# Dealing TensorE fill to attention steps by each step's own matmul work

## The chip, the cores and the metric

One Trainium2 chip; the kernel runs on one core. The metric is device time in microseconds (us) of one execution, median of several. PE is TensorE, DVE is VectorE, ACT is ScalarE, POOL is GpSimd and SP is SyncE. TensorE's clock has two levels here, 2.4 GHz (granted clock 1.00) and 1.2 GHz (0.50).

## The reference

Thresholded attention for 2 batches x 8 heads, sequence 576, head width 64; its output, 1152 tokens of 512, passes through two layers of experts, 8 and then 4, each expert 512 to 1024 to 512 and computed for all tokens.

```python
def _attn_ref(q, k, v, tau):
    scores = scale * np.matmul(q, k.transpose(0, 1, 3, 2))
    thresh = np.max(scores, axis=-1, keepdims=True) - tau
    scores = np.where(scores >= thresh, scores, -1000000000.0)
    scores = scores - np.max(scores, axis=-1, keepdims=True)
    attn = np.exp(scores)
    attn = attn / (np.sum(attn, axis=-1, keepdims=True) + 1e-09)
    return np.matmul(attn, v).astype(np.float32)
...
    for e in range(E):                       # first layer, P: gate, normalized by rows and columns 8 times
        h = np.maximum(x @ w1[e], 0.0)
        out += P[:, e:e + 1] * (h @ w2[e])
...
    for e in range(E):                       # second layer, p: given probabilities, normalized by row
        h = np.maximum(x @ w1[e], 0.0)
        out += p[:, e:e + 1] * (h @ w2[e])
```

## The kernel before

The queries of the 16 head-and-batch pairs are cut into 72 **units** of up to 128 queries. `Attention.step` (L396) is one step of a software pipeline and works on several units at once: at step time `t` it transposes the normalized weights of unit t-2, masks and reduces unit t and t+1, computes the scores of unit t+2, and, where a group of 320 or 256 queries is complete, multiplies its weights with the values (`mix`, nine matmuls into a PSUM tile `pv`). The program's order on each engine is the order in which this Python code is written; nothing reorders it. In this text a step has the number k of the unit that it transposes, so k = t-2, and it begins with PE's transposes of that unit (tiles `et` and `er`, L313 and L315).

In a step, PE has: five transposes; **fill, phase 0**; scores (L271, four matmuls, eight in a few steps); `pv` (L355, L357) in some steps; **fill, phase 1**. ACT has: the copy of `et` out of PSUM (`hi`, L320, and of a finished `er`, L322), the copy of a finished `pv` (`out`, L374), the relu of a fill group that ended in phase 0 (L474), the exponential (L291), the relu of a group that ended in phase 1, and then preparation for coming heads (casts of keys, values, queries and weights: L71, L239, L240, L96). DVE has: mask (L295), maximum (L276), three small ones, then `lo` (L330 and, for a finished `er`, L333), then what lies in the list `later`: the `rest` of `pv` (L377), and `hl` of a fill group (L477).

**Fill** is expert work of the first layer that is ready before all heads are (`expert_fill`, L457): tokens of batch 0 first, 256 and then 320 columns at a time. It is a generator that yields after each **piece**. A layer-1 group (L468) has three pieces of four matmuls and accumulates in one PSUM bank; its bank comes free when ACT's relu and DVE's `hl`, which subtracts the relu's result from the sum, have read it. A layer-2 group (L495) has twelve pieces of two matmuls 512 columns wide; its bank comes free with ACT's copy L499. `pv` of attention takes its tile from the same pool `ps_m`, which has **two banks**; the other six banks are scores (four), `et` (one) and `er` (one). A `pv` bank comes free with `out` on ACT and `rest` on DVE, which stand in the step after the one that filled it.

Fill begins at k=18 and stops about k=33, when its first batch of work is used up; the second batch begins at k=38. The dealing is in `fill` and `pull` (L563 to L583): `pull(3)` in phase 0 of every step; in phase 1, when a group is still open or the step has no `pv`, more pieces up to 3 (or 4 in the second batch).

Of the kernel before, what the change touches and what calls it, by code (L numbers as in the profile page):

```python
# [22 lines left out]
NT = N // P  # L23
HS = S // 2
BIG = 3.0e38
RA1, RA2 = 3, 4


@with_exitstack
def attention_two_moe_kernel(ctx, tc, qP, kP, qT, kT, vp, tau, wg, w1, w1s, w2, dp, m2w1s, m2w2, out):  # L30
# [80 lines left out]
    class Attention:  # L111
# [5 lines left out]
        def __init__(self, pl, ps_s, ps_t, ps_r, ps_m):  # L117
            self.pl, self.ps_s, self.ps_t, self.ps_r, self.ps_m = pl, ps_s, ps_t, ps_r, ps_m
            self.units, self.heads = [], []
            self.t = -2  # L120
            self.work = {}
            self.later, self.late = [], []
            self.iq = self.iv = self.lq = self.lv = 0
            self.xf = {}
            self.eth = pl.tile([P, 5, 640], F32R, name="eth")
            self.e32 = pl.tile([P, 5, 512], F32, tag="etl", name="e32")
            self.etl = None
            self.qz = [pl.tile([P, 3 * D], F32R, name=f"qz{i}") for i in range(2)]
            for z in self.qz:
                V.tensor_scalar(z[:, D:2 * D], ident[:, :D], 0.0, None, op0=ALU.mult)  # L130
# [208 lines left out]
        def mix(self, g, part):  # L339
            hd, n, c = g["head"], g["n"], slice(g["c"], g["c"] + g["n"])  # L340
            if part == 0:
                g["pv"] = self.ps_m.tile([P, 512], F32, tag="mm", name="pv")
            pv = g["pv"]
            if hd["exact"]:
                r0 = (hd["h"] % 2) * D
                for kt in self.parts(hd)[part]:
                    k = P if kt < 4 else D
                    T.matmul(pv[r0:r0 + D, :n], lhsT=hd["v"][:k, kt], rhs=self.e32[:k, kt, c], start=kt == 0,  # L348
                             stop=kt == 4)
                if part == 2:  # L350
                    self.lv -= 1
            elif part == 0:
                vf = hd["vs"].rearrange("p a b c -> p a (b c)")
                for kt in range(4):
                    T.matmul(pv[:, :n], lhsT=vf[:, kt], rhs=self.etl[:, kt, c], start=kt == 0, stop=False)  # L355
                for kt in range(5):
                    T.matmul(pv[:, :n], lhsT=vf[:, kt], rhs=self.eth[:, kt, c], start=False, stop=kt == 4)  # L357

        def out(self, g):
            hd, n, pv, pl = g["head"], g["n"], g["pv"], self.pl  # L360
            h, t0 = hd["h"], hd["b"] * S + g["q0"]
            r0 = (h % 2) * D
            r, kt, c = slice(r0, r0 + D), h // 2, slice(t0, t0 + n)
            if hd["exact"]:
                A.copy(xh[r, kt, c], pv[r, :n])
                self.later.append(lambda: V.tensor_tensor(xl[r, kt, c], pv[r, :n], f(xh[r, kt, c]), op=ALU.subtract))
                return

            key = hd["h"] // 2, g["n"]
            if key not in self.xf:  # L370
                self.xf[key] = pl.tile([P, n], F32, tag=f"xf{n}", name="xf", bufs=1)
            xf = self.xf[key]
            o = slice(D - r0, 2 * D - r0)
            A.copy(xf[r, :n], pv[o, :n])  # L374

            def rest():
                V.tensor_tensor(xf[r, :n], pv[r, :n], xf[r, :n], op=ALU.add)  # L377
                if "half" in self.xf.setdefault(key + ("n",), {}):
                    del self.xf[key], self.xf[key + ("n",)]
                    self.late.append(lambda: split(A, G, xh[:, kt, c], xl[:, kt, c], xf[:, :n]))  # L380
                else:
                    self.xf[key + ("n",)]["half"] = True

            self.later.append(rest)
# [11 lines left out]
        def step(self, fill, side):  # L396

            us, t = self.units, self.t
            un = lambda i: us[i] if 0 <= i < len(us) else None
            self.load()  # L400
            nxt, a, d, x, c, z, y = (un(t + i) for i in (2, 1, 0, -2, -3, -4, -5))
            if x:
                self.turn(x)
            if d:
                self.mask(d)
            if a:
                self.top(a)
            if d:
                self.guard(d)
            if a:  # L410
                self.line(a)
            if d:
                self.norm(d)
            for part, u in ((2, y), (1, z), (0, c)):
                for g in u["mix"] if u else ():
                    if g["head"]["exact"]:
                        self.mix(g, part)
            if x:
                self.hi(x)
            for u, late in ((z, False), (y, True)):  # L420
                for g in u["mix"] if u else ():
                    if late == (g["head"]["exact"] and g["head"]["h"] < H - 1):
                        self.out(g)
            fill(0, bool(c and c["mix"]))
            if a:
                self.exp(a)
            if x:
                self.lo(x)
            if nxt:
                self.scores(nxt)  # L430
            self.run(self.later)
            for g in c["mix"] if c else ():
                if not g["head"]["exact"]:
                    self.mix(g, 0)
            fill(1, bool(c and c["mix"] or z and z["mix"]))
            self.run(self.late)
            for w in self.work.pop(t, ()):
                w()
            side()
            self.t += 1  # L440
            return self.t < len(us) + 5
# [15 lines left out]
    def expert_fill(hp, w, n0, n, cols, dst, tail, q0, later, free):  # L457

        hs = []
        for ft in range(FT):
            wh, wl = w.w1(ft)
            ph = bank()
            ops = [(wl, xh), (wh, xl), (wh, xh)]
            for i, (a, x) in enumerate(ops):
                for kt in range(KT):
                    T.matmul(ph[:, :n], lhsT=a[:, kt * P:(kt + 1) * P], rhs=x[:, kt, n0:n0 + n],  # L468
                             start=i == 0 and kt == 0, stop=i == 2 and kt == KT - 1)
                if i < 2:  # L470
                    yield 2 - i
            hh = hp.tile([P, n], F32R, tag="hh", name="hh", bufs=FT)
            hl = hp.tile([P, n], F32R, tag="hl", name="hl", bufs=FT)
            A.activation(hh, ph[:, :n], AF.Relu)  # L474

            def low(hh=hh, hl=hl, ph=ph, ft=ft):
                V.scalar_tensor_tensor(hl, ph[:, :n], 0.0, f(hh), op0=ALU.max, op1=ALU.subtract)  # L477
                if tail is not None:
                    for h, to in zip((hh, hl), tail):
                        for q, c in enumerate((0, n - 32)):  # L480
                            G.tensor_scalar(to[:, ft, (q0 + q) * 32:(q0 + q + 1) * 32], f(h[:, c:c + 32]), 1.0, 1.0,
                                            op0=ALU.mult, op1=ALU.mult)

            later.append(low)
            hs.append((hh, hl))
            free(1)
            yield 0
        for t, c in cols:
            py = bank()
            i = 0  # L490
            for ft in range(FT):
                (hh, hl), (wh, wl) = hs[ft], w.w2(ft)
                hh, hl = (x[:, c:c + P] for x in (hh, hl)) if t < NT - 1 else (x[:, ft] for x in tail)
                for x, a in ((hl, wh), (hh, wl), (hh, wh)):
                    T.matmul(py, lhsT=x, rhs=a, start=i == 0, stop=i == 3 * FT - 1)  # L495
                    i += 1
                    if i % 2 == 0 and i < 3 * FT:
                        yield 12 - i // 2
            A.copy(dst[t], py)  # L499
            yield 0  # L500
        free(FT)

    def keep(n):
        pass
# [9 lines left out]
    with ExitStack() as att:  # L514
# [45 lines left out]

        left, spent = [0], [0]

        def pull(n, end=True):  # L563

            for i in range(n):
                if not todo or at.t <= todo[0][0] or (left[0] == 1 and not end):
                    return i
                left[0] = next(todo[0][1], -1)
                if left[0] < 0:
# [3 lines left out]
                    return i + 1  # L573
            return n

        def fill(phase, busy):
            if phase == 0:
                if 0 <= at.t < nA0 - 3 and at.t % 2 == 0:
                    room[0] -= 1
                    cook()  # L580
                spent[0] = pull(3)
            elif left[0] or not busy:
                pull(max((RA1 if at.t < nA1 + 3 else RA2) - spent[0], 0), True)  # L583

        while at.step(fill, side):
            pass
# [168 lines left out]
    def scale():  # L755

        for t in (0, 1, 2, 3, 4, 5, 6, 7, 8):
            e = int(t > 3)
            V.tensor_scalar(acc[t], acc[t], p1[:, t, e:e + 1], None, op0=ALU.mult)
            if t < 4:  # L760
                V.scalar_tensor_tensor(acc[t], y1[t], p1[:, t, 1:2], acc[t], op0=ALU.mult, op1=ALU.add)
# [324 lines left out]
```

## Time and profile before

| what | value |
|---|---|
| median of 3 runs | 1345.97 us (1344.51 to 1347.28) |
| the profiled execution's own time | 1345.91 us |
| its span in the profile | 1344.1 us (1.8 us outside it) |
| PE busy | 1316.8 us, 98% of the span |
| DVE, ACT, POOL busy | 50%, 42%, 52% of the span |
| steps k=18 to 32 | 65.18 to 115.17 us |
| steps k=33 to 37 | 115.17 to 130.23 us |
| steps k=38 to 70 | 130.23 to 245.40 us |

A step's start is the start of its first transpose L313 on PE. The steps with fill are a sixth of the span; the rest is expert work, whose matmuls follow one another closely.

### The profile page before, as it was taken

To read this page: it belongs to the slowest core of one execution; us is meant where nothing else is said; L and a number is where in the kernel's file an instruction comes from. 1 tells how busy PE (TensorE), PEld (TensorE's weight loads), DVE (VectorE), ACT (ScalarE), POOL (GpSimd) and SP (SyncE) were. 2 spreads that over 40 slices of the span, in tenths; PEclk is the share of its full clock that TensorE was granted. 3 is DMA by queue.
4 is the path that set the end of the run, shared out by engine and by line. 5 is a ranking of instruction groups with operands and counts; after the bars stand their busy time and mean duration, and the time that the engine had idled before them with its cause. 6 is when DMAs were issued, how large, how long until landed. Compare 5 with 4: busy or idle time off the path is not lost.

```text
span 1344.1 us, 20909 instructions
## 1 busy us (share of the span) xinstructions
PE 1316.8 (98%) x7777; PEld 1164.7 (87%) x7777; DVE 670.9 (50%) x1526; ACT 567.4 (42%) x1300; POOL 696.8 (52%) x837
## 2 busy tenths in 40 slices
PE   8998999999999999999999999999899999999998
PEld 5697988899889889898898989888789889898987
DVE  5798888356863434343343433434334334343343
ACT  6887786333444324242332423335434233242321
POOL 6886975442875335434543643544963454364330
PEclk9999999999999999999999999999999999999999
DMA  5542330100321112011111201101101111120101
GB/s 156 162 125 65 104 94 17 32 24 25 103 71 39 48 40 63 24 56 48 31 50 47 63 25 56 48 25 55 48 24 56 48 32 50 46 63 25 32 9 63
DMA packets 42054, 73.58 MB, mean 55 GB/s; under 512 B 5088, under 2 KB 10336, under 8 KB 41952
## 3 DMA queue, kind: packets, MB, share of 16 engines
q1 hardware_dynamic: 41664, 71.96, 18.0%
q8 instruction: 61, 1.00, 0.3%
q14 instruction: 41, 0.34, 0.1%
q10 hardware_dynamic: 288, 0.28, 0.1%
HBM read 69.86 MB, written 2.36 MB: 54 GB/s over the span
## 4 chain that ended last, share of the span: by engine, by line
PE 90%; DVE 3%; ACT 3%; POOL 3%; issue 1%; DMA 0%; POOLq 0%; ACTq 0%; DVEq 0%
PE mm L1003 38%; PE mm L893 33%; PE mm L468 5%; PE mm L495 5%; PE sc L271 2%; PE et L313 2%; PE pv L348 2%; PE pv L357 1%; PE pv L355 1%; DVE ex L295 1%; DVE etl L330 1%; POOL wl L76 1%; DVE st L276 1%; ACT ex L291 0%; ACT eth L320 0%
## 5 line engine op out<-in xcount | busy, mean ns | idle before, releaser
L1003 PE MATMUL mm<-wh,hs 128*128 128x512 f32 x1344 | 435.4, 397 | 2.0 <-DVE hs L869 2.0
L76 POOL TENSOR_TENSOR wl<-raw,wh 128x512 fp32r<-128x512 f32 x154 | 199.3, 1307 | 337.1 <-ACT wh L71 335.0
L1003 PEld LDWEIGHTS mm<-wh,hs 128*128 128x128 f32 x1344 | 252.3, 188 | 64.1 <-DVE hs L869 8.3
L1011 DVE SCALAR_TENSOR_TENSOR acc<-mm,p,acc 128x512 f32<-128x512 f32 x181 | 135.7, 750 | 300.7 <-PE mm L1003 300.7
L1003 PE MATMUL mm<-wl,hs 128*128 128x512 f32 x672 | 264.1, 393 | 0.0
L898 ACT COPY s<-mm 128x288 f32<-128x288 f32 x84 | 33.6, 401 | 450.4 <-PE mm L893 450.4
L869 DVE SCALAR_TENSOR_TENSOR hs<-mm,hs 128x288 fp32r<-128x288 f32 x252 | 114.8, 456 | 103.5 <-ACT hs L868 103.1
L1003 PEld LDWEIGHTS mm<-wl,hs 128*128 128x128 f32 x672 | 126.6, 188 | 27.2
L893 PE MATMUL mm<-xh,wl 128*128 128x288 f32 x672 | 144.3, 296 | 2.4 <-ACT w L898 1.4
L893 PE MATMUL mm<-xl,wh 128*128 128x288 f32 x672 | 143.8, 295 | 0.0
L893 PE MATMUL mm<-xh,wh 128*128 128x288 f32 x672 | 143.8, 295 | 0.0
L76 POOL TENSOR_TENSOR wl<-ws,wh 128x512 fp32r<-128x512 f32 x88 | 115.8, 1319 | 36.4 <-ACT wh L71 26.7
L868 ACT ACTIVATE hs<-mm 128x288 fp32r<-128x288 f32 x252 | 104.2, 414 | 69.5 <-DVE mm L920 64.7
L893 PEld LDWEIGHTS mm<-xh,wl 128*128 128x128 f32 x672 | 110.1, 189 | 7.0 <-ACT w L898 1.9
L893 PEld LDWEIGHTS mm<-xh,wh 128*128 128x128 f32 x672 | 108.1, 188 | 0.0
L893 PE MATMUL mm<-xth,wl 128*128 128x288 f32 x504 | 107.9, 295 | 0.0
L893 PEld LDWEIGHTS mm<-xl,wh 128*128 128x128 f32 x672 | 107.9, 188 | 0.0
L893 PE MATMUL mm<-xth,wh 128*128 128x288 f32 x504 | 107.7, 295 | 0.0
L893 PE MATMUL mm<-xtl,wh 128*128 128x288 f32 x504 | 107.7, 295 | 0.0
L875 POOL TENSOR_SCALAR ht<-hs 128x128 fp32r<-128x128 f32 x168 | 49.7, 302 | 111.1 <-ACT hs L868 96.2
L71 ACT CAST wh<-raw 128x512 fp32r<-128x512 f32 x154 | 95.7, 623 | 13.5 <-PE mm L893 10.4
L631 POOL TENSOR_TENSOR ws<-raw 128x512 f32<-128x512 f32 x44 | 57.6, 1309 | 53.9 <-DMA raw<-in_w1s 31.0
(172 smaller groups left out, 2299.2 us busy)
## 6 DMA issues: line engine op xcount, KB each, us to landing
raw<-in_w SPq DMA_DIRECT2D x88, 256.0 KB, 3.0
raw<-in_w1s SPq DMA_DIRECT2D x56, 256.0 KB, 2.7
raw<-in_m2w1s SPq DMA_DIRECT2D x32, 256.0 KB, 2.7
raw<-in_m2w SPq DMA_DIRECT2D x32, 256.0 KB, 2.9
kr<-in_kT SPq DMA_DIRECT2D x22, 288.0 KB, 2.9
vr<-in_vp SPq DMA_DIRECT2D x24, 160.0 KB, 2.3
qr<-in_qT SPq DMA_DIRECT2D x8, 288.0 KB, 2.8
out_y<-acc SPq DMA_DIRECT2D x8, 256.0 KB, 2.0
```

What stands on the lines that cost most here:

```text
L71: A.copy(hi, src)
L76: el.tensor_tensor(lo, src, f(hi), op=ALU.subtract)
L468: T.matmul(ph[:, :n], lhsT=a[:, kt * P:(kt + 1) * P], rhs=x[:, kt, n0:n0 + n], start=i == 0 and kt == 0, stop=i == 2 and kt == KT - 1)
L495: T.matmul(py, lhsT=x, rhs=a, start=i == 0, stop=i == 3 * FT - 1)
L631: G.tensor_tensor(s, a, b, op=op)
L868: A.activation(hh, src, AF.Relu)
L869: V.scalar_tensor_tensor(hl, src, 0.0, f(hh), op0=ALU.max, op1=ALU.subtract)
L875: G.tensor_scalar(tail[j][:, :, q:q + 32], f(side[s][j][:, :, 2 * P:]), 1.0, 1.0, op0=ALU.mult, op1=ALU.mult)
L893: T.matmul(m, lhsT=w[:, (2 * g + kt) * P:(2 * g + kt + 1) * P], rhs=operand(u, kt, lo), start=first and j == 0, stop=j == len(ops) - 1, sk ...
L898: A.copy(z[name], m)
L1003: T.matmul(py, lhsT=hs[x][:, k, o:o + P], rhs=w, start=n == 0, stop=n == 3 * HF - 1)
L1011: V.scalar_tensor_tensor(acc[t], py, s, acc[t], op0=ALU.mult, op1=ALU.add)
```

## The change

A step gets a budget in place of a fixed number. At phase 0 the program adds up the step's own PE work in nanoseconds (`own`: 550 for the transposes, 530 for each group of scores, four for each column of `pv`) and adds (3300 - own)/480 pieces to what the step before left over, of which at most one piece is carried. Up to 3 whole pieces are dealt in phase 0 and the rest in phase 1. A new group is not begun while more than one of the two banks has users whose releasing instructions are not yet written (`later` and the new counter `open`). Two lines keep the scaling of a result from being written before the fill that makes that result (`written`).

```diff
-RA1, RA2 = 3, 4
+STEP, PIECE = 3300, 480
...
             if part == 0:
                 g["pv"] = self.ps_m.tile([P, 512], F32, tag="mm", name="pv")
+                self.open += 1
...
             hd, n, pv, pl = g["head"], g["n"], g["pv"], self.pl
+            self.open -= 1
...
-            fill(0, bool(c and c["mix"]))
+            own = 550 + 530 * len(nxt["q"] if nxt else ()) + sum(4 * g["n"] for g in (c["mix"] if c else ()))
+            fill(0, bool(c and c["mix"]), own)
...
-        def pull(n, end=True):
+        def pull(n):
...
-                if not todo or at.t <= todo[0][0] or (left[0] == 1 and not end):
+                if not todo or at.t <= todo[0][0] or (left[0] == 0 and len(at.later) + at.open > 1):
...
-        def fill(phase, busy):
+        def take(n):
+            n = min(n, int(spent[0])) if todo and at.t > todo[0][0] else 0
+            while n > 0:
+                k = pull(n)
+                n, spent[0] = (n - k if k else 0), spent[0] - k
+
+        def fill(phase, busy, own=0):
             if phase == 0:
...
-                spent[0] = pull(3)
-            elif left[0] or not busy:
-                pull(max((RA1 if at.t < nA1 + 3 else RA2) - spent[0], 0), True)
+                if todo and at.t > todo[0][0]:
+                    spent[0] = min(spent[0], 1) + (STEP - own) / PIECE
+                    take(3)
+            else:
+                take(6)
...
+            while (False, t) not in written or t < 4 and (True, t) not in written:
+                yield 1
```

The same instructions run as before. On PE their order differs from step k=18 to the first L893; the six 512-column matmuls of the first batch that stood in k=33 stand before it, and k=38 to 70 hold seven more pieces of 320 columns, which leave the steps behind k=70.

PE, step k=20, before: transposes, one whole layer-1 group, scores, and the next step's transposes.

```order
109 L313 MATMUL et<-ident,ex 128x128 x4
110 L315 MATMUL er<-ident,ex 64x128
111 L468 MATMUL mm<-xh,wl 128x256 x4
112 L468 MATMUL mm<-xl,wh 128x256 x4
113 L468 MATMUL mm<-xh,wh 128x256 x4
114 L271 MATMUL sc<-kh,qs 128x288 x2
115 L271 MATMUL sc<-kl,qs 128x288 x2
116 L313 MATMUL et<-ident,ex 128x128 x4
```

PE, the same step of the changed kernel (its lines are one to four higher: L472 is the layer-1 piece).

```order
108 L314 MATMUL et<-ident,ex 128x128 x4
109 L316 MATMUL er<-ident,ex 64x128
110 L472 MATMUL mm<-xh,wh 128x256 x4
111 L272 MATMUL sc<-kh,qs 128x288 x2
112 L272 MATMUL sc<-kl,qs 128x288 x2
113 L472 MATMUL mm<-xh,wl 128x256 x4
114 L472 MATMUL mm<-xl,wh 128x256 x4
115 L472 MATMUL mm<-xh,wh 128x256 x4
116 L472 MATMUL mm<-xh,wl 128x256 x4
117 L314 MATMUL et<-ident,ex 128x128 x4
```

Before, the group begins behind the transposes; now the end of an older group stands there, and two groups (a group's first piece is `xh,wl`) begin behind the scores in the same step. `pv` of step 19 and that older group hold the two banks when the step begins.

PE, step k=42, before.

```order
299 L313 MATMUL et<-ident,ex 128x128 x4
300 L315 MATMUL er<-ident,ex 64x128
301 L468 MATMUL mm<-xh,wl 128x320 x4
302 L468 MATMUL mm<-xl,wh 128x320 x4
303 L468 MATMUL mm<-xh,wh 128x320 x4
304 L271 MATMUL sc<-kh,qs 128x288 x2
305 L271 MATMUL sc<-kl,qs 128x288 x2
306 L313 MATMUL et<-ident,ex 128x128 x4
```

PE, step k=42 of the changed kernel.

```order
301 L314 MATMUL et<-ident,ex 128x128 x4
302 L316 MATMUL er<-ident,ex 64x128
303 L472 MATMUL mm<-xh,wh 128x320 x4
304 L272 MATMUL sc<-kh,qs 128x288 x2
305 L272 MATMUL sc<-kl,qs 128x288 x2
306 L472 MATMUL mm<-xh,wl 128x320 x4
307 L472 MATMUL mm<-xl,wh 128x320 x4
308 L472 MATMUL mm<-xh,wh 128x320 x4
309 L472 MATMUL mm<-xh,wl 128x320 x4
310 L314 MATMUL et<-ident,ex 128x128 x4
```

The step holds five pieces in place of three; one stands ahead of the scores, and the first piece of the next group stands behind them, in the step whose DVE `rest` frees the bank of step 41's `pv`.

PE, step k=66 of the changed kernel: the last piece of a layer-2 group (L499), then at once the first piece of a layer-1 group, which takes the bank of the group that has just ended, once ACT's copy (in this step, behind `hi` and `out`) has read it; before, k=66 held layer-2 pieces alone.

```order
553 L314 MATMUL et<-ident,ex 128x128 x4
554 L316 MATMUL er<-ident,ex 64x128
555 L499 MATMUL mm<-wl,hh 128x512
556 L499 MATMUL mm<-wh,hh 128x512
557 L472 MATMUL mm<-xh,wl 128x320 x4
558 L272 MATMUL sc<-kh,qs 128x288 x2
```

## Rows read from the trace of the kernel before

**Rows 1.** The page, busy time by engine and shares of the chain that ended last.
```profile
PE 1316.8 (98%) x7777; PEld 1164.7 (87%) x7777; DVE 670.9 (50%) x1526; ACT 567.4 (42%) x1300; POOL 696.8 (52%) x837
...
PE 90%; DVE 3%; ACT 3%; POOL 3%; issue 1%; DMA 0%; POOLq 0%; ACTq 0%; DVEq 0%
```

**Rows 2.** Busy time by stretch (x counts), then TensorE clock, DMA share and GB/s.
```profile
core 0: us, PE busy (x) PEld busy (x) DVE busy (x) ACT busy (x) POOL busy (x), PEclk, DMA share, GB/s
65.18:115.17 49.99, 47.64 (x340) 44.84 (x340) 45.66 (x128) 39.87 (x81) 39.39 (x47) 1.00 0.40 114
115.17:130.23 15.06, 10.97 (x75) 9.60 (x74) 13.62 (x39) 11.04 (x22) 9.33 (x11) 1.00 0.23 62
117.75:130.23 12.48, 8.39 (x59) 7.44 (x59) 11.10 (x32) 8.92 (x18) 7.32 (x9) 1.00 0.27 75
130.23:245.40 115.17, 112.37 (x769) 103.23 (x770) 99.02 (x273) 84.88 (x166) 83.05 (x128) 1.00 0.21 63
274.20:277.60 3.40, 3.40 (x18) 3.35 (x16) 0.61 (x2) 0.65 (x2) 0.00 (x0) 0.50 0.00 0
```

**Rows 3.** Timeline of PE, two short steps and a long one (start, duration, idle before).
```profile
81.43 0.60 PE L313 MATMUL et<-ident,ex 128*128 128x128 f32 x4
...
85.64 0.63 PE L313 MATMUL et<-ident,ex 128*128 128x128 f32 x4 [1.53 <-POOL qz L244]
...
88.77 0.75 PE L355 MATMUL pv<-etl,vhl 128*128 128x320 f32 x4
...
90.09 0.60 PE L313 MATMUL et<-ident,ex 128*128 128x128 f32 x4
...
90.55 0.72 PE L468 MATMUL mm<-xh,wl 128*128 128x256 f32 x4
...
91.58 0.64 PE L468 MATMUL mm<-xh,wh 128*128 128x256 f32 x4
92.06 0.43 PE L271 MATMUL sc<-kh,qs 128*128 128x288 f32 x2
...
92.60 0.60 PE L313 MATMUL et<-ident,ex 128*128 128x128 f32 x4
```

**Rows 4.** Timeline of ACT, then of DVE, in the step that starts at 81.43.
```profile
82.00 0.46 ACT L71 CAST xh<-xf 128x320 fp32r<-128x320 f32 x1
...
83.67 0.61 ACT L96 CAST wh<-raw 128x512 fp32r<-128x512 f32 x1
84.20 0.58 ACT L320 CAST eth<-et 128x512 fp32r<-128x512 f32 x1
...
84.81 0.69 DVE L330 TENSOR_TENSOR etl<-et,eth 128x512 fp32r<-128x512 f32 x1 [0.64 <-ACT eth L320]
```

**Rows 5.** Timeline of ACT, then of DVE, in the step that starts at 90.09.
```profile
90.72 0.59 ACT L320 CAST eth<-et 128x512 fp32r<-128x512 f32 x1 [0.88 <-PE et L313]
...
91.34 0.69 DVE L330 TENSOR_TENSOR etl<-et,eth 128x512 fp32r<-128x512 f32 x1 [0.44 <-ACT eth L320]
92.07 0.42 DVE L333 TENSOR_TENSOR eth<-er,eth 64x256 fp32r<-64x256 f32 x1
92.52 0.48 DVE L377 TENSOR_TENSOR xf<-pv,xf 64x320 f32<-64x320 f32 x1
92.92 0.41 DVE L477 SCALAR_TENSOR_TENSOR hl<-mm,hh 128x256 fp32r<-128x256 f32 x1
```

**Rows 6.** Timeline of PE, then of DVE, in the step that starts at 245.40.
```profile
245.40 0.60 PE L313 MATMUL et<-ident,ex 128*128 128x128 f32 x4
...
245.86 0.82 PE L468 MATMUL mm<-xh,wl 128*128 128x320 f32 x4
...
247.11 0.75 PE L468 MATMUL mm<-xh,wh 128*128 128x320 f32 x4
248.52 0.82 PE L468 MATMUL mm<-xh,wl 128*128 128x320 f32 x4 [0.66 <-DVE xf L377]
...
247.88 0.49 DVE L377 TENSOR_TENSOR xf<-pv,xf 64x320 f32<-64x320 f32 x1
```

**Rows 7.** Costliest PE group by line, 65.18:115.17, then 130.23:245.40, with idle time.
```profile
L313 PE MATMUL et<-ident,ex 128*128 128x128 f32 x61 | 9.4, 274 | 3.2 <-POOL qz L244 1.5 <-DVE etl L330 1.4 <-POOL qs L241 0.3
...
L313 PE MATMUL et<-ident,ex 128*128 128x128 f32 x133 | 20.2, 273 | 2.8 <-DVE etl L330 2.8
```

**Rows 8.** Groups of DVE by line, 130.23:245.40, then durations of line L499 on ACT.
```profile
L295 DVE SCALAR_TENSOR_TENSOR ex<-sc,st,ex 128x576 f32<-128x576 f32 x32 | 26.1, 814 | 1.4 <-ACT ex L291 0.4
L276 DVE TENSOR_REDUCE st<-sc 128x1 f32<-128x576 f32 x31 | 23.3, 753 | 0.0
...
L499 ACT COPY y<-mm x2: 586/586/586, 222.3 to 232.6; 128x512 f32<-128x512 f32 x2
```

More of the change, by code (lines that the diff above doesn't have):

```diff
@@ L122, in __init__ @@
             self.later, self.late = [], []
+            self.open = 0
             self.iq = self.iv = self.lq = self.lv = 0
@@ L499, in expert_fill @@
             A.copy(dst[t], py)
+            written.add((dst is y1, t))
             yield 0
         free(FT)
+    written = set()
     def keep(n):
```

## The prediction

> **What bounds the kernel now.** I read the page first: PE is busy for 1316.8 us, 98% of the span, and the chain that ended last is PE for 90% [rows 1]. Over the whole span, then, only about 27 us are idle on PE, and a change of order that keeps every instruction can give or take no more than waits. Next I read the stretches by windows, since the average hides where the waits are [rows 2]. In k=18 to 32 PE is busy 47.64 of 49.99 us and DVE 45.66; in k=38 to 70 PE 112.37 of 115.17 and DVE 99.02; in between, k=33 to 37, PE has almost no fill and DVE sets the pace (13.62 of 15.06). The reader is to see that DVE is close behind PE in all three: a PE that waits loses time, and a DVE that is asked for something early will not have it.
>
> Then I read what PE waits for. By line nearly all recorded idle time stands before the transposes L313: 3.2 us in the first stretch and 2.8 us in the second [rows 7]. The timeline shows how it comes about [rows 3]. The steps that start at 81.43 and 90.09 issue the same list on PE: transposes, three pieces, scores. One takes 85.64 - 81.43 = 4.21 us, the other 92.60 - 90.09 = 2.51. In the first, ACT reaches `hi` only at 84.20, behind the casts that begin at 82.00, so DVE's `lo` begins at 84.81 and ends at 85.50; the next transposes, which need the single `et` buffer, start at 85.64 [rows 4]. The idle time is labelled with a POOL instruction, but the end of `lo` is what fits. Short steps run ahead, long ones (88.77 adds 1.32 us of `pv`) let ACT and DVE catch up. That is what evened-out steps would address.
>
> **The change part by part.** *Work.* Nothing is added or removed; PE's sum is the same. From [rows 3]: transposes 90.55 - 90.09 = 0.46; three pieces 92.06 - 90.55 = 1.51; scores 92.60 - 92.06 = 0.54; so a piece of 256 columns is about 0.5, and from [rows 6] the first of 320 starts at 245.86 and the third at 247.11, about 0.6 each. Adding such unit times over the pieces of each stretch, I get 46.8 us of PE work in k=18 to 32 (3.2 us of waits, as recorded) and 107.9 in k=38 to 70, which leaves 7.3 us of waits: more than the 2.8 recorded [rows 7], because a modelled end covers part of each gap. I take 7.3, the value that favours the change.
>
> *What goes away.* If all steps are of one length, the waits before transposes can go: 3.2 us in k=18 to 32 and, of the 7.3, all but 0.8 at k=38, which the change doesn't reach: 6.5. Against that, the six 512-column matmuls that leave k=33 (six at about 0.24, 1.46 us) no longer fill a step that DVE paces, so they cost their time: +1.46.
>
> *What comes in.* The two banks that fill and `pv` share. Before, a new group begins behind the transposes, and its bank's last reader stood a step earlier, so the bank was free. In the changed order a group often begins late in the same step whose DVE or ACT instructions free its bank. The program's order keeps that legal; it doesn't make the reader early. When does the reader end? The step at 90.09 shows it with little queued ahead: `hi` begins at +0.63, `lo` at +1.25, L333 at +1.98, `rest` at +2.43 and ends at 93.00, +2.91; `hl` ends at +3.24 [rows 5]. And one place of the trace already has this order, the step at 245.40: its second group could start at 247.70, 0.59 behind 247.11, but starts at 248.52, just behind the end of `rest` at 248.37 [rows 6]. That is a wait of 0.8 by starts, 0.66 recorded. It is the row that prices the new waits.
>
> So each new wait is: end of the reader, less the time at which PE arrives. At k=20 PE arrives behind transposes, one piece and scores, 0.46 + 0.48 + 0.54 = 1.48, and `rest` ends at 2.91: 1.45. At k=42 it arrives at 1.6 by the same sum with a 320-column piece: about 1.4. At k=66 it arrives at 0.93 (transposes, two matmuls of 512) and needs ACT's copy: `hi` until +1.22, `out` about 0.4, copy 0.586 [rows 8], so 2.25: 1.35. I went through every first matmul of a group or `pv` in this way:
>
> - behind `rest`: k=20 1.45, 22 0.15, 25 1.0, 42 1.4, 44 0.35, 53 0.7, 55 0.5, 57 0.45, 69 1.3: 7.3 us;
> - behind `hl` of a group that ended in this step or just before: k=21 0.9, 24 0.4 + 0.8, 41 0.7, 43 0.6, 56 0.15, 58 0.4, 59 0.55, 68 0.9, 70 0.7: 6.1;
> - behind an ACT copy of a layer-2 result: k=48 0.9, 51 0.2, 62 1.15, 66 1.35: 3.6;
> - scores behind the mask, which takes 0.81 [rows 8], at k=19: 0.6.
>
> That is 17.6 us, 5.3 of them up to k=25 and 12.3 from k=41 on. At k=71 one piece less stands ahead of the group that already waits, and `rest` comes at the same time: +0.6.
>
> *Sum.* k=18 to 37: 5.3 - 3.2 + 1.46 = +3.6. k=38 to 70: 12.3 - 6.5 = +5.8. k=71: +0.6. Together +10.0 us. On the profiled execution's own 1345.91 us, 0.06 under the median, that is 1355.9.
>
> *Bounds.* With each new wait at the low end (readers 0.2 to 0.4 earlier: 3.3 and 9.6) the sum is 1.6 + 3.1 + 0.2 = +4.9, 1350.8. If the early waits don't go at all where steps stay uneven, it is 5.3 + 1.46 + 12.3 + 0.6 = +19.7; but a PE that has just waited in mid-step lets ACT and DVE catch up, so I take half of the 9.7 us as gone at worst: +14.8, 1360.7. The scale instructions held back by `written` run on DVE long before its result is needed and are covered by expert matmuls that wait for nothing of theirs: 0; at worst one late tile, 0.75, the length of L276 of like width [rows 8].
>
> *A rule beside it.* PE here has two banks for three kinds of groups, and the trace shows the cost of taking a bank before its reader is done: 0.66 us idle before 248.52 [rows 6]. The Trainium skill (Perfetto Trace Analysis, section Matmuls) says that independent groups should rotate through different banks, so that the evacuation of one overlaps the next group's matmuls. Before, the fixed order mostly did so; by the rule the change, which puts two or three group starts into some steps with two banks, loses that overlap. The trace agrees at that one place.
>
> **The rivals.**
>
> *Evened steps pay, faster.* If `rest`, `hl` and the copies land before PE arrives, the new waits vanish and only the old ones go. For it: DVE has room (99.02 of 115.17), and an ACT that gets its order at even distances reaches `hi` sooner than at 84.20 [rows 2, 4]. Against it: the chain `hi`, `lo`, `rest` takes 2.9 us even with nothing queued [rows 5]. At the bound, -3.2 + 1.46 - 6.5 = -8.2; with half of the second stretch's old waits gone and the first's all, -1.7 - 3.3 = -5.0: 1340.9. It decides if `rest` ends within about 1.6 us of the step's first transpose at k=20, 42 and 69. Chance 0.13.
>
> *One wait for another, no change.* DVE paces the stretches: it is busy 45.66 of 49.99 and 99.02 of 115.17, and the rest of its time is mostly hand-overs with ACT. Then PE's wait before `pv` or fill is the wait it would have had before the next transposes, and the stretch takes what DVE takes: 1346. For it: 91% busy in the first stretch. Against it: 86% in the second, where 12.3 us of new waits meet at most 6.5 old ones, and a PE that stands in mid-step delays the scores and transposes on which DVE works next. Chance 0.15, the change not doing what it says included.
>
> *The clock, slower still.* The granted clock fell to 0.50 in 274.20 to 277.60, behind a stretch of tiny matmuls, and cost about half of those 3.4 us [rows 2]; in the stretch without fill it stayed at 1.00 with PE busy 8.39 of 12.48 us. The change makes that stretch a step longer and empties it by 1.46 us. If the clock fell there, PE's 8.39 us of work would take up to twice as long, of which DVE's pace hides a part: up to +6 on top, 1362. For it speaks only the longer stretch; against it, 1.00 throughout before. Chance 0.05. [...]
>
> **How the numbers follow.** The main case has 0.67, the clock 0.05, no change 0.15, faster 0.13. The likeliest gives 1355.9, its own range 1350.8 to 1360.7. For eight times in ten the range has to take in the no-change case and the lower part of the main one, and leaves out the faster case and most of the clock: 1344 to 1361. About 0.2% (2.7 us) is what a measurement can tell here: faster means under 1343.3, slower over 1348.7. Chances 0.13, 0.15 and 0.72.
>
> **What would show it.** In the changed kernel's profile: PE idle in mid-step, before layer-1 pieces, `pv` and layer-2 pieces, released by DVE `rest`, `hl` or by ACT's copy, 1 us or more at k=20, 25, 42, 62, 66 and 69, and 12 us or more of such waits by starts in all; idle before L313 much smaller than 3.2 + 2.8; k=18 to 37 longer by about 4 us and k=38 to 70 by about 10, of which the seven pieces more (at 0.6, 4.2 us) are 4; L495 in none of k=33 to 37. Behind k=71 the kernel should take back those 4.2 us and be otherwise as long as now. I am wrong if idle before fill and `pv` stays under 3 us (readers earlier than I read), if new waits appear but the DVE windows don't lengthen (one for one), or if the expert stretches behind take a different time, which I count at nothing.

## The result and the profile after

The changed kernel takes 1362.17 us, median of 4 runs (1361.21 to 1363.57); the kernel before, timed again beside it, 1346.02. The ratio is 1.0115, 95% interval 1.0104 to 1.0127: 16 us slower. The forecast was 1355.9, slower, in a range up to 1361.0. The direction and the mechanism came as forecast, the size did not: the median lies 1.2 us above the range.

The profiled execution took 1363.57, of which 1361.8 is its span. Its page, busy time by engine and shares of the chain that ended last, beside [rows 1]:

```profile
PE 1319.6 (97%) x7777; PEld 1165.2 (86%) x7777; DVE 675.3 (50%) x1526; ACT 568.8 (42%) x1300; POOL 698.0 (51%) x837
...
PE 87%; DVE 6%; ACT 4%; POOL 2%; issue 2%; DMA 0%; ACTq 0%; POOLq 0%; DVEq 0%
```

The instructions are the same in number, and PE's busy time has hardly moved. DVE has gone from 3% to 6% of the chain: PE waits for it more often. Windows of the changed kernel say where (k=18 to 32, k=33 to 37, k=38 to 70, then two short stretches, then the start of the expert layer), beside [rows 2]:

```profile
core 0: us, PE busy (x) PEld busy (x) DVE busy (x) ACT busy (x) POOL busy (x), PEclk, DMA share, GB/s
66.85:122.22 55.37, 50.67 (x345) 46.11 (x346) 45.71 (x128) 39.91 (x81) 39.47 (x47) 1.00 0.36 103
122.22:138.42 16.20, 11.19 (x69) 9.60 (x68) 13.63 (x40) 11.54 (x23) 9.36 (x11) 0.89 0.21 59
138.42:265.74 127.32, 117.14 (x797) 107.85 (x798) 100.64 (x275) 85.77 (x168) 85.01 (x137) 1.00 0.19 57
23.50:27.00 3.50, 3.50 (x12) 2.34 (x12) 2.46 (x9) 2.46 (x5) 3.32 (x5) 0.52 0.71 214
126.00:129.50 3.50, 3.15 (x15) 2.67 (x13) 3.47 (x11) 2.37 (x5) 2.73 (x3) 0.51 0.43 121
```

Against the 49.99, 15.06 and 115.17 us of before, the three stretches have grown by 5.38, 1.14 and 12.15. Of the last, 4.2 are the seven pieces more, so 7.95 are loss. The first step with fill begins at 66.85 for 65.18, 1.67 later, in a part that the change leaves alone. There the clock was at 0.51 to 0.52 from 23.5 to 27.0, which it was not in the kernel before, nor in most of the kernels below (x_a3 and z_b have a like fall near 23 us); I put it down to this execution and not to the change, which starts at k=18.

The line with most idle time before [rows 7], the transposes, in k=18 to 32 and k=38 to 70:

```profile
L314 PE MATMUL et<-ident,ex 128*128 128x128 f32 x60 | 9.0, 273 | 0.8 <-DVE etl L331 0.8
...
L314 PE MATMUL et<-ident,ex 128*128 128x128 f32 x133 | 20.1, 272 | 0.9 <-DVE etl L331 0.9
```

That is what evening out was to do: 3.2 and 2.8 us have become 0.8 and 0.9, and both stand in the first step of their stretch, k=18 and k=38, where they stood before the change too. What PE waits for instead, by the chain of waits in k=38 to 70 (engine, line, what ended the wait: us, times, longest):

```profile
PE mm L472 <- DVE xf L380: 4.0, 5, 1.3
PE pv L357 <- DVE hl L481: 2.6, 5, 0.7
PE mm L472 <- ACT y L503: 1.2, 1, 1.2
PE mm L499 <- ACT y L503: 1.0, 1, 1.0
PE et L314 <- DVE etl L331: 0.9, 1, 0.9
PE mm L499 <- ACT acc L503: 0.7, 1, 0.7
```

All but one of these are waits for a bank of the fill and `pv` pool. The step k=20, timeline of PE and then of DVE, shows the first of them:

```profile
73.98 0.60 PE L314 MATMUL et<-ident,ex 128*128 128x128 f32 x4
...
75.26 0.43 PE L272 MATMUL sc<-kl,qs 128*128 128x288 f32 x2
77.03 0.72 PE L472 MATMUL mm<-xh,wl 128*128 128x256 f32 x4 [1.34 <-DVE xf L380]
...
76.40 0.48 DVE L380 TENSOR_TENSOR xf<-pv,xf 64x320 f32<-64x320 f32 x1
```

PE could have begun the group 1.54 us into the step, at 75.52; `rest` ends at 76.88, +2.90, and the group begins at +3.05: 1.5 us lost, for the 1.45 forecast. At k=66 the releaser is ACT. PE, then ACT:

```profile
243.21 0.60 PE L314 MATMUL et<-ident,ex 128*128 128x128 f32 x4
...
243.98 0.40 PE L499 MATMUL mm<-wh,hh 128*128 128x512 f32 x1
245.54 0.85 PE L472 MATMUL mm<-xh,wl 128*128 128x320 f32 x4 [1.16 <-ACT y L503]
...
243.90 0.59 ACT L321 CAST eth<-et 128x512 fp32r<-128x512 f32 x1 [1.94 <-PE et L314]
244.51 0.37 ACT L377 COPY xf<-pv 64x256 f32<-64x256 f32 x1
244.90 0.59 ACT L503 COPY y<-mm 128x512 f32<-128x512 f32 x1
```

The copy ends at 245.49, +2.28, forecast +2.25. ACT had been idle for 1.94 us before `hi`: the reader is late because of what stands ahead of it in the step, not because ACT is full.

### The profile page after: what moved, and what is told of

The parts are those of the page before. It is cut to its first block, busy times and chain, and to the rows that moved or that the text cites. A ratio compares the mean times of both kernels' runs of the same rounds, so it can differ in the third digit from the quotient of the medians.

```text
span 1361.8 us, 20925 instructions
## 1 busy us (share of the span) xinstructions
PE 1319.6 (97%) x7777; PEld 1165.2 (86%) x7777; DVE 675.3 (50%) x1526; ACT 568.8 (42%) x1300; POOL 698.0 (51%) x837
## 4 chain that ended last, share of the span: by engine, by line
PE 87%; DVE 6%; ACT 4%; POOL 2%; issue 2%; DMA 0%; ACTq 0%; POOLq 0%; DVEq 0%
PE mm L1020 37%; PE mm L910 31%; PE mm L499 5%; PE mm L472 4%; PE sc L272 2%; PE et L314 2%; PE pv L350 2%; PE pv L359 1%; PE pv L357 1%; DVE ex L296 1%; ACT eth L321 1%; DVE etl L331 1%; DVE st L277 1%; DVE hs L886 1%; POOL wl L76 0%
## 5 line engine op out<-in xcount | busy, mean ns | idle before, releaser
L1020 PE MATMUL mm<-wh,hs 128*128 128x512 f32 x1344 | 435.6, 396 | 2.2 <-DVE hs L886 1.9
L1020 PEld LDWEIGHTS mm<-wh,hs 128*128 128x128 f32 x1344 | 252.3, 188 | 64.7 <-DVE hs L886 8.8
L1020 PE MATMUL mm<-wl,hs 128*128 128x512 f32 x672 | 264.1, 393 | 0.0
L1020 PEld LDWEIGHTS mm<-wl,hs 128*128 128x128 f32 x672 | 126.5, 188 | 27.1
L910 PE MATMUL mm<-xh,wl 128*128 128x288 f32 x672 | 144.5, 296 | 3.3 <-ACT w L915 2.3
L910 PE MATMUL mm<-xh,wh 128*128 128x288 f32 x672 | 143.8, 295 | 0.0
L910 PE MATMUL mm<-xl,wh 128*128 128x288 f32 x672 | 143.8, 295 | 0.0
L910 PEld LDWEIGHTS mm<-xh,wl 128*128 128x128 f32 x672 | 110.1, 188 | 8.2 <-ACT w L915 3.0
L910 PE MATMUL mm<-xth,wl 128*128 128x288 f32 x504 | 108.1, 295 | 0.6 <-DVE t L930 0.6
L910 PEld LDWEIGHTS mm<-xh,wh 128*128 128x128 f32 x672 | 108.1, 188 | 0.0
L910 PEld LDWEIGHTS mm<-xl,wh 128*128 128x128 f32 x672 | 107.9, 188 | 0.0
L910 PE MATMUL mm<-xth,wh 128*128 128x288 f32 x504 | 107.7, 295 | 0.0
L910 PE MATMUL mm<-xtl,wh 128*128 128x288 f32 x504 | 107.7, 295 | 0.0
```

Source lines behind the costliest of these rows:

```text
L910: T.matmul(m, lhsT=w[:, (2 * g + kt) * P:(2 * g + kt + 1) * P], rhs=operand(u, kt, lo), start=first and j == 0, stop=j == len(ops) - 1, sk ...
L1020: T.matmul(py, lhsT=hs[x][:, k, o:o + P], rhs=w, start=n == 0, stop=n == 3 * HF - 1)
```

## Experiments

**Late starts taken out.** Two variants keep the budget and forbid what I hold to be the cause, in two ways; a third puts late starts into the kernel before without any budget. Theory 1: the place of a group's start, relative to the instructions that free its bank, costs the time. Rival: the budget costs, by giving long steps little fill and short ones much.

```diff
# e1_start0, against the changed kernel
-(left[0] == 0 and len(at.later) + at.open > 1)
+(left[0] == 0 and (not begin or len(at.later) + at.open > 1))    # begin: phase 0 only
-spent[0] = min(spent[0], 1) + (STEP - own) / PIECE;  take(3)
+spent[0] = min(spent[0], 2) + (STEP - own) / PIECE;  take(4)
# e4_safe, against the changed kernel; rec["t"]: the step in which a bank's last reader was written
+def held():
+    return at.t < len(at.units) + 5 and len(at.rel) > 1 and at.rel[-2].get("t", at.t) >= at.t
-(left[0] == 0 and len(at.later) + at.open > 1)
+(left[0] == 0 and (len(at.later) + at.open > 1 or held()))
-min(spent[0], 1)
+min(spent[0], 3)
# e2_late_fixed, against the kernel before
-if ... (left[0] == 1 and not end):
+if ... (left[0] == 0 and len(at.later) + at.open > 1):
-spent[0] = pull(3)
-elif left[0] or not busy:
+spent[0] = pull(1)
+else:
```

Expected of e1_start0: 

> The changed kernel, with a new group begun only in phase 0 (phase 1 only continues an open one); up to two pieces are carried and four dealt in phase 0, so that the amount of fill in k=38 to 70 is about that of before (35 pieces of 320 for 36, 96 matmuls of 512). Theory 1 (what costs is a group that begins in the step whose instructions free its bank): the waits behind the scores that the changed kernel's trace shows at k=20, 25, 42, 53, 55, 57 and 69 (7.5 us) vanish and those of pv behind hl stay in part; the time falls to between 1346 and 1353, and the first L910 to first L1020 stretch goes back to 11.2 us since the fill left over covers the gate again. Rival (the budget itself costs: long steps are now empty of fill and short ones full, so DVE and ACT set another pace): the waits only move, and the time stays at 1358 or above.

Expected of e4_safe: 

> The changed kernel with the budget kept (up to three pieces carried) and one rule more: a group begins only if the instructions that free its bank were written in an earlier step. Late starts are allowed where that holds; the amounts are those of before (36 pieces of 320 in k=38 to 70) or a little more (46 matmuls of 512 in k=18 to 32 for 42). Theory 1: PE's waits before fill nearly vanish, those before pv stay at k=41, 59, 68 (about 2 us), the transposes wait less than before; 1341 to 1349. Rival (the budget costs): 1356 or more, with the waits now before the transposes or scores.

Expected of e2_late_fixed: 

> The kernel before, with its fixed number of pieces and no budget, but one piece dealt in phase 0 and the others in phase 1, and the changed kernel's rule on when a group may begin: groups then end, and most new ones begin, behind the scores. Theory 1 (the place of the start costs, not the budget): slower than before though nothing is dealt by work, since most starts stand at about +1.0 and need an hl that ends at about +3 or an hl late in the step before: some 12 starts at 1.5 to 2 us less the old waits of about 10, 1355 to 1366. Rival (the budget costs): within 3 us of before, 1343 to 1349.

| kernel | median us | before beside it | ratio, 95% interval |
|---|---|---|---|
| e1_start0 | 1355.48 | 1347.39 | 1.0065 (1.0051 to 1.0079) |
| e4_safe | 1350.77 | 1347.39 | 1.0028 (1.0017 to 1.0039) |
| e2_late_fixed | 1412.48 | 1347.39 | 1.0485 (1.0470 to 1.0499) |

With starts held until their bank's reader stands a step back, the loss of 16 us falls to 3.4, budget and all; that is 1.8 us above the range I gave. Starts in phase 0 alone leave 8.1, above what I expected too: `pv` still waits 4.5 us for `hl` there, and the banks of layer-2 groups 2.1 us for ACT's copy. And late starts without a budget are four times worse than the change, 65 us; I had counted twelve starts and expected 1355 to 1366. (e2_late_fixed also deals in phase 1 of steps with `pv`, and holds three pieces more in k=38 to 70, 1.8 us.) The longest sums among its waits of PE, k=18 to 70:

```profile
PE mm L471 <- DVE hl L480: 24.7, 13, 3.5
PE pv L357 <- DVE hl L480: 12.9, 12, 1.8
PE et L314 <- DVE etl L331: 6.0, 7, 1.3
```

The number of waiting starts was nearly right (13 for 12), their price was not: nearly 2 us each in the mean and up to 3.5, and `pv` and the transposes wait besides. No budget deals here, so this loss is the place's. In its timeline the clock was at its lower level several times besides, the window of k=38 to 70 showing 0.94 in the mean, so a part of the 65 us is that.

**The bank itself.** The starts can stay where the change puts them if the pool has a third bank. To free one I left out a piece of the computation in all four kernels of this set.

```diff
# x_b2, x_b3 (order of before), x_a2, x_a3 (order of the changed kernel)
-eg["er"] = self.ps_r.tile([P, 512], F32, tag="er", name="er")
-T.transpose(eg["er"][:D, c:c + P], exf[:, 4 * P:], ident)
-A.copy(eth[:D, 4, ...], eg["er"][:D, :eg["n"]])
+A.copy(eth[:D, 4, ...], u["exf"][:D, :eg["n"]])          # and the same in lo
-ps_m: 2 banks
+ps_m: 3 banks                                            # x_b3, x_a3 only
```

Expected of x_b2: 

> The order of before without the er transposes: L315 is left out, and ACT's and DVE's copies of er (L322, L333) read 64 rows of the weights in SBUF instead, so the last 64 keys get wrong weights; that frees a PSUM bank, which stays unused here. Control for the three others. Both theories: 1344 to 1348, at most 2 us less than before for the 72 missing transposes.

Expected of x_b3: 

> As x_b2 (same computation left out), with the freed bank given to the pool of fill and pv, which then has three; order of before. Theory 1 (banks): its waits before were nearly all before the transposes, which a third bank doesn't touch: within 2 us of x_b2. Rival (DVE and ACT pace, banks are not the point): the same.

Expected of x_a2: 

> The changed kernel with the same computation left out as in x_b2 and two banks for fill and pv, the freed bank unused. Both theories: the loss of the changed kernel remains, 12 to 16 us over x_b2.

Expected of x_a3: 

> As x_a2 with three banks for fill and pv; order of the changed kernel. Theory 1: with three banks a group's bank was freed a step earlier at nearly every late start, so the waits of fill and pv behind rest, hl and copies fall from some 17 us to under 5 and the time to within 5 us of x_b3 (what is left being the uncovered gate, some 2 us, and the emptier k=33 to 37). Rival (the budget makes steps that DVE and ACT can't follow): the waits come back before the transposes and scores, and the loss stays above 10 us.

| us | two banks | three banks |
|---|---|---|
| order of before | 1349.07 | 1344.39 |
| order of the changed kernel | 1365.47 | 1344.54 |

Against the kernel before these are ratios of 1.0018 (1.0009 to 1.0027), 0.9984 (0.9975 to 0.9993), 1.0145 (1.0131 to 1.0159) and 0.9988 (0.9979 to 0.9997). With two banks the changed order costs 16.4 us, with three 0.15. This is the plainest of the runs: the same instructions in the same order, and one bank more takes back the whole loss. (In the profile of x_a2 the clock also fell once more, from 75.5 to 78.9 in k=20, so a part of its loss is that.)

Three expectations of this set were off. The 16.4 us lie just above the 12 to 16 I gave for x_a2. The control x_b2 is 2.9 us slower than before, where I had said at most 2 faster. And the third bank is worth 4.7 us to the order of before, where I had said within 2. The traces show what the last two have in common. The copy of the last 64 keys in `lo` now has both its sources in SBUF, and takes longer. In the kernel before and in x_b2 (durations in ns, least, median, most):

```profile
L333 DVE TENSOR_TENSOR eth<-er,eth x24: 417/419/552, 68.0 to 247.4; 64x256 fp32r<-64x256 f32 x16, 64x384 fp32r<-64x384 f32 x8
```

```profile
L329 DVE TENSOR_TENSOR eth<-ex,eth x24: 418/643/1668, 68.8 to 250.4; 64x256 fp32r<-64x256 f32 x16, 64x384 fp32r<-64x384 f32 x8
```

`rest` stands behind it on DVE. So the control waits for banks ten times in k=18 to 70, 0.7 us and less each and 3.3 in all, where the kernel before has one such wait of 0.2 in its list; it is these that the third bank takes away. That fits the 2.9 us, though no run takes the copy alone. Against the kernel before, x_b3 is 1.8 us faster. Both orders of the set have the long copy, so the comparison of 16.4 with 0.15 stands.

The waits of PE in x_a2 and in x_a3, k=18 to 70:

```profile
PE mm L468 <- DVE xf L376: 7.2, 6, 2.2
PE sc L272 <- DVE ex L296: 4.5, 5, 1.4
PE pv L353 <- DVE hl L477: 4.4, 7, 0.8
```

```profile
PE sc L272 <- DVE ex L296: 7.2, 8, 1.7
PE et L312 <- DVE etl L327: 3.6, 4, 1.0
PE mm L468 <- DVE xf L376: 2.2, 2, 1.4
```

With three banks the waits of layer-1 pieces for `rest` fall from 7.2 to 2.2 us and those for `hl` leave the list, as expected; the scores now wait for the mask, so DVE is next. Windows of k=38 to 70 in x_b3 and then in x_a3 show that the even dealing does pay in this set once banks suffice:

```profile
130.50:243.91 113.41, 108.36 (x736) 99.93 (x736) 100.58 (x273) 85.34 (x166) 84.62 (x128) 1.00 0.22 64
```

```profile
134.28:248.08 113.80, 110.67 (x763) 104.01 (x764) 102.51 (x275) 85.93 (x168) 87.07 (x137) 1.00 0.21 64
```

Nearly the same length with seven pieces (4.2 us) more in it: 3.8 us won. It is given back in two places that are looked at next: the gate, and k=33 to 37.

**The amount, and the gate.** I read the fill that the change uses up early as cover, too. Behind the attention steps the gate of the first expert layer runs as a chain on DVE with fill on PE beside it; its last products, the scaled sums, go to DVE just ahead of the expert layer's own first instructions. The stretch from the first L893 that reads `xth` (L910 now) to the first L1003 (L1020 now), in the kernel before and then in the changed kernel:

```profile
333.06:341.13 8.07, 8.07 (x62) 8.07 (x61) 4.99 (x13) 6.12 (x16) 6.45 (x5) 1.00 0.22 59
```

```profile
348.08:358.33 10.25, 8.71 (x63) 8.18 (x61) 9.36 (x17) 5.95 (x16) 7.24 (x5) 1.00 0.15 41
```

PE's work there is the same; DVE is busy 9.36 us for 4.99, and PE stands still for 1.5 us. The scaling of the sums (L759, now L776) in these two windows, before and after:

```profile
L759 DVE TENSOR_SCALAR acc<-acc,p 128x512 f32<-128x512 f32 x2 | 0.9, 484 | 0.0
```

```profile
L776 DVE TENSOR_SCALAR acc<-acc,p 128x512 f32<-128x512 f32 x6 | 5.3, 878 | 0.0
```

Six of them in place of two now run among the expert layer's own instructions. The next run uses a smaller budget, so that as much fill as in the kernel before is left.

```diff
# e5_step3200, against the changed kernel
-STEP, PIECE = 3300, 480
+STEP, PIECE = 3200, 480
```

Expected: 

> The changed kernel with a budget of 3200 ns for 3300: 36 pieces of 320 columns in k=38 to 70 (43 in the changed kernel, 36 before), 44 matmuls of 512 in k=18 to 32 and 4 behind them; late starts as before (13). Theory on the gate (the changed kernel used up fill that before covered the gate's chain on DVE): the stretch from the first TensorE matmul of expert layer 1 on xth to the first L1020 goes back from 10.2 to 8.1 us. Theory 1 (late starts): the waits in k=18 to 70 stay, so the time is 1356 to 1361, 2 to 6 us under the changed kernel. Rival (amount is what costs): the time is within 5 us of before.

It took 1365.56 us, ratio 1.0148 (1.0134 to 1.0162). Its windows of k=38 to 70 and of the stretch at the gate:

```profile
139.22:266.55 127.33, 113.55 (x769) 103.72 (x770) 99.14 (x273) 85.11 (x166) 83.64 (x129) 1.00 0.19 57
354.23:362.30 8.07, 8.07 (x62) 8.07 (x61) 4.99 (x13) 6.12 (x16) 6.48 (x5) 1.00 0.18 56
```

The gate is back at 8.07, as (within 0.01) in e1_start0, e4_safe and x_b3, which also leave about as much fill as before, while x_a2 and x_a3 with the changed amounts have 10.22 and 10.24. So the 2.2 us go with the amount of fill that is left: they are the cover. But the time went up by 3.4 where I expected 2 to 6 less: k=38 to 70 are as long with seven pieces less, since other starts now fall on their releasers (layer-1 pieces wait 9.7 us for `rest` up to k=71, for 6.5 in the changed kernel, and `pv` 8.3 us for `hl`, for 4.4). The rival, that the amount costs, is out for the bulk of the loss; and the price of a late start depends on where it falls, by several us in all.

**Three banks in full.** The last set computes everything and takes `er` from the pool only in a group's last step, which needs a fifth `ex` buffer; to pay for it the prefetch gave up one buffer each of `raw` and `vr`.

```diff
# z_b (order of before), z_a (changed kernel), z_c (z_a with STEP = 3200)
+eg.setdefault("exs", []).append((u["c"] - eg["c0"], exf))
+if u["last"]:
+    eg["er"] = self.ps_m.tile([P, 512], F32, tag="mm", name="er")
+    for c, e in eg["exs"]:
+        T.transpose(eg["er"][:D, c:c + P], e[:, 4 * P:], ident)
-ps_m 2, ps_r 1;  ex 4, raw 3, vr 3
+ps_m 3;          ex 5, raw 2, vr 2
```

Expected of z_b: 

> A full computation with three banks for fill and pv in the order of before: er takes its tile from the same pool, and its two or three transposes are done together in the group's last step; five ex buffers for four, two raw and two vr buffers for three. Theory 1: as with the bank freed by leaving er out, a little faster than before: 1341 to 1346. Rival (er in the pool takes the bank away again, or fewer buffers delay loads): 1346 to 1352.

Expected of z_a: 

> The order of the changed kernel with the same three banks and buffers: theory 1: the changed kernel's loss falls from 16 to between 0 and 5 us over before, the gate's 2 us among them: 1344 to 1351. Rival (er in the pool takes a bank when it is needed): above 1354.

Expected of z_c: 

> As z_a with a budget of 3200 ns, so that fill is left for the gate. If both causes are as I think (banks, and fill spent that the gate needs), this is the fastest of the family: 1339 to 1346. Rival: no faster than z_b.

They took 1358.57, 1362.75 and 1365.17 us, ratios 1.0089 (1.0073 to 1.0105), 1.0116 (1.0100 to 1.0131) and 1.0145 (1.0132 to 1.0159): all three slower than the kernel before, and none is the better kernel that I looked for. z_b lies above both of the ranges that I gave it, z_a in its rival's, and z_c is slower than z_b. The first window of z_b, up to its k=18, and what PE waited for most in it:

```profile
0.00:80.52 80.52, 64.17 (x261) 39.47 (x261) 43.65 (x145) 51.29 (x97) 49.88 (x59) 0.89 0.40 124
```

```profile
PE pv L349 <- DMA vr<-in_vp: 7.8, 3, 3.1
```

k=18 begins 15 us later than in the kernel before. 7.8 us of that are waits for the values, which the kernel before doesn't have; PE is busy 64.17 us there for 57.40, at a mean clock of 0.89 for 1.00. In k=38 to 70, with enough loads ahead, z_b needs 113.88 us for 115.17, and z_a 118.01 for the changed kernel's 127.32. Less the 4.2 us of its seven more pieces, z_a takes what z_b takes: with three banks and the whole computation the changed order costs nothing in these steps, though it gains nothing either. So sharing the bank helps there, and the buffers that I took for it cost more than it gave. No run has three banks and three `vr` buffers, so what the third bank is worth to a whole kernel that keeps its loads stays open.

## Why the prediction was too low

**The new waits: right.** Read by starts from the changed kernel's timeline, step by step, they come to 6.0 us in k=18 to 32 (5.3 forecast) and 12.6 in k=38 to 70 (12.3). k=25, 42, 48, 62, 66 and 69 measure 1.0, 1.4, 0.9, 1.1, 1.3 and 1.3 against 1.0, 1.4, 0.9, 1.15, 1.35 and 1.3. k=53 was the worst miss, 1.1 for 0.7. The step at 245.40 [rows 6] was the row to price them by, and the runs with three banks show that the bank is the cause.

**"What goes away": too much.** This step failed in its size. I let all old waits go but 0.8. By starts, k=38 to 70 have 15.2 us of waits now (127.32 less 107.9 + 4.2), 7.9 more than before, for the 5.8 forecast; k=18 to 32 lost 5.38 - 1.46 = 3.9 for the 2.1 of the sum. Together that is about 3.9 us more than forecast. About 1.0 of it is new waits; the other 2.9 are old waits that stayed. Those before the transposes did go, but for the first step of each stretch: 0.9 at k=38, which I had kept, and 0.8 at k=18, which I had let go. And k=38 also waits behind its transposes, in both kernels alike: 0.20 and 0.1 us as recorded, for `xh` and `xl`, about 0.9 by starts. The rest is short waits spread over the steps.

**The emptied steps and the clock.** The +1.46 for k=33 to 37 assumed that they stay as long as they were. They grew from 15.06 to 16.20. In this stretch the clock fell to 0.51 from 126.0 to 129.5, which I gave one chance in twenty. It happened in five kernels that have less fill there than the six matmuls of before: the changed kernel, x_a2 and x_a3 with none, e4_safe with two and e5_step3200 with four. They need 15.9 to 17.1 us for these steps. The kernel before, e2_late_fixed, x_b2 and x_b3 with all six, and e1_start0 with four, kept 1.00 there and need 14.6 to 15.4. (The three kernels with the pool's `er`, z_b with all six too, fell there as well, after falls already in the steps before k=18.) As e1_start0 and e5_step3200 have the same four, the missing fill doesn't decide it alone, and what does stays open. The Trainium skill (TensorE: Matmul & The Clock Gate, Part 1: The HAM clock gate) says that how busy PE has been of late sets the clock; the trace agrees in that the fall at 126.0 came in steps without fill, but doesn't tell those two runs apart. So this rival was no alternative but came along, at about 1 us for the changed kernel, as an estimate from the growth of 1.14; the forecast of up to 6 was far too high, and DVE is busy 13.63 of the 16.20 us there. Nor does the fall belong to every execution: the fastest of the four runs, 1361.21 us, has a mean granted clock of 1.000, the profiled one 0.997. On the other side, the low clock of 274.20 to 277.60 behind the gate's tiny matmuls [rows 2] did not come in the profiled execution of the changed kernel, which gives about 1.7 us back, half of the 3.4.

**The expert stretches "which I count at nothing".** The step that failed outright. I held the scale instructions to be covered, 0 in the sum and 0.75 at worst. The change uses up fill that covered the gate's chain, so they reach DVE among the first instructions of the expert layer: 10.25 us for 8.07, 2.2 us.

The sum of the profiled executions: 6.5 in k=18 to 37, 7.95 in k=38 to 70, about 0.5 at k=71, 2.2 at the gate, less 1.7 for the clock, is 15.5; with 1.67 from the start of this execution 17.1 of the 17.7 between the two spans, and 0.5 more stands behind the gate's stretch. The median of the four runs is 1.4 below the profiled one.

**The rivals and the range.** "Evened steps pay" failed by its condition (`rest` within 1.6 us): it ends at +2.90. What it says of the dealing is half true: with three banks that is worth 3.8 us in k=38 to 70 without `er`, and nothing between z_b and z_a. "One wait for another" is out by the 16 us, and by the 20.9 us between x_a2 and x_a3: DVE can follow, it was not pacing. The range was too narrow at the top because of the terms that I counted at nothing. Its upper bound allowed for 4.85 us of old waits that stay, more than the 2.9 that did; but it held nothing for the 1.1 us by which k=33 to 37 grew, and not even the 0.75 for the scale instructions, which cost 2.2.

## What to carry to other kernels

When work is moved within an in-order pipeline, write down for each tile that it takes who frees it and in which step, and place it a step behind: equal steps help only as far as the buffers reach. The waits of a place that already has the new pattern price it well; count them place by place. And fill that is spent early is missing as cover later, so look at what ran beside it in the next stage.

## What was not expected of the hardware

Two different levels of the clock in k=33 to 37, with little between the kernels: the kernel before held 1.00 with PE busy 10.97 of 15.06 us [rows 2], the changed kernel, with six matmuls fewer there, fell to 0.51 for 3.5 us with 11.19 of 16.20, which includes the time at the low level. With the same four matmuls there, e1_start0 held 1.00 and e5_step3200 fell.

And a small subtraction on DVE got longer with both sources in SBUF (x_b2): 643 ns in the median, 418 to 1668, for 419 with one of them in PSUM (the kernel before). What makes the longest ones so long isn't shown.
